# Last stage of an attention and two-layer kernel on one core: conversion steps a turn behind their producers, block sums in finer steps

## The chip, the core and the metric

The kernel runs on one core of a Trainium2 chip. A core has a matrix engine (TensorE, PE in the profile, with PEld for its weight loads), VectorE (DVE), ScalarE (ACT), GpSimd (POOL) and SyncE (SP, which here only issues DMAs). Each engine works through its own list of instructions in order, and waits at an instruction until the semaphores that it needs have been raised; what stands behind a waiting instruction on the same engine waits too. The metric is the device time of one execution in microseconds.

## What is computed

The reference is a block-causal attention (4 batches, 8 heads, 576 positions), a two-layer mixing network on its output, and a third part, which is the last stage of the kernel:

```python
xn = (x - mu) / np.sqrt(var + 1e-06) * g_ln
ch = np.maximum(xn @ w_ch1, 0.0) @ w_ch2
return (x + ch)
```

There `x` has 2304 rows of 512, `w_ch1` is 512 x 2048 and `w_ch2` 2048 x 512, all in float32. The reference draws `w_ch1` and `w_ch2` as float32 inputs, so the kernel has to prepare them on the chip.

## The kernel before, in words

Every matrix product is made with three passes: each float32 operand is split into a high part that PE takes as it is and a low part (the rest), and PE adds high x high, high x low and low x high.

The last stage takes `w_ch1` and `w_ch2` in 8 chunks of 256 hidden units (c = 0 to 7), with two weight buffers `W[c % 2]`. The rows are in five groups: four of 512 rows in two pairs, P = (0, 3) and Q = (2, 1), and a group Z of 256 rows (number 4). For a chunk and a group, `em_c1` makes the hidden units (PE into `ph` tiles in PSUM, five buffers; ACT writes the high part of `h1`, DVE the low part at line 659), and `em_c2` multiplies `h1` with `w_ch2` (PE into `po` tiles, three buffers) and adds on DVE into `acc` (line 818). `em_c2` of a group stands behind `em_c1` of the next one.

For a pair of 512-row groups `em_c1s` replaces the two `em_c1`: it makes the pair's products with seven block products in place of eight (42 matmuls of 512 columns where two `em_c1` take 48). It needs four block sums of the inputs (`SF[0]` to `SF[3]`, 1 MB each, made once for each pair by `sum_forms` on DVE, ACT and POOL) and four of the weights (`TF[c]`, made anew for each chunk by `forms`). There is room for one pair's sums, so they are written to DRAM (`s_scr`), and `reload(i)` fetches those of the next pair into `SF[i]` once PE has read it. Inside `em_c1s` the PSUM tile `b` is read by ACT (`act(z, b)`) and then added to by a later product, so PE waits for that read.

The weights come in through SP in four jobs a chunk (`load_split`): `load` (DMA of raw bytes into one of two `raw8` buffers, which `forms` takes turns in too), `above` and `below` (two ACT operations that take the exponent out; the tile `a1` of `above` has one buffer, which `bits` gives back), `expo` (a subtraction, on POOL in this stage), `bits` (DVE, line 134), `high` (ACT copy) and `low` (POOL subtraction). `Convert.step`, called by `tick` between PE's pieces, moves each job that is under way one step on and starts one; `expo` and `bits` are one step. A turn is what one such call emits.

The chunks run: c = 0 and 1 with `em_c1` throughout; c = 2 with `em_c1s` for P only and `em_c1` for Z and Q; from c = 3 on with `em_c1s` for both pairs and `em_c1` for Z between them. P's sums are made during c = 1, Q's during c = 2. The weights of chunk c + 1 are converted during chunk c. The lists of DMAs are the order of SP, which has one queue; the order of all engines is that in which the code emits.

Of the kernel before, what the change touches and what calls it, by code (L numbers as in the profile page):

```python
# [32 lines left out]
def attention_moe_kernel(ctx, tc, raw_d, dup_d, raw0_d, dup0_d, v_d, v0_d, msk_d, mz_d, vec_d, eye_d, wk_d, wv_d, wr_d, wc1_d, wc2_d, out_d):  # L33
# [181 lines left out]
    T = {}  # L215
# [371 lines left out]
    def chunk_jobs(c):  # L587
        L, kept = [], []
        for k in (0, 2):
            w = wc1_d[128 * k:128 * k + 256, CF * c:CF * c + CF].rearrange("(a p) n -> p a n", a=2)  # L590
            L.append(load_split(w, lambda i, k=k: W[c % 2][0][i][:, k:k + 2], kept))
        for k in range(2):
            r0 = CF * c + 128 * k
            L += pieces(wc2_d[r0:r0 + 128], lambda i: W[c % 2][1][i], k, DM)
        if c > 1:

            z = []

            def forms():
                (b11, b12), (b21, b22) = [[st["a2"].rearrange("p (a n) -> p a n", a=2)[:, :, o:o + 128] for o in (0, 128)] for st in kept]  # L600
                raw = stg2.tile([128, 4096], I8, name="raw8")
                z.append(raw.bitcast(F32).rearrange("p (i a n) -> p i a n", i=4, a=2))
                z1, z2, z3, z4 = [z[0][:, i] for i in range(4)]
                for out, in0, in1 in ((z1, b12, b11), (z3, b22, b12), (z2, b22, z1), (z4, b21, z2)):
                    tt(out=out, in0=in0, in1=in1, op=ALU.subtract)

            L[2][2] += (forms,)
            L[2][3] = (L[2][3], lambda: act(TF[c][0], z[0]))
            L[2][4] = (L[2][4], lambda: sub(nc.gpsimd, TF[c][1], z[0], TF[c][0]))
        return L  # L610
# [62 lines left out]
    def sum_forms(pr, pool):  # L673

        (g0, g1) = pr
        v, g = nc.vector, nc.gpsimd
        st = {}

        def block(G, h, k):
            return [x[:, k].bitcast(F32) for x in quarter(G, h)]  # L680

        def op(eng, out, in0, in1, op=ALU.subtract):
            eng.tensor_tensor(out=out, in0=in0, in1=in1, op=op)  # L683

        def temp(n):
            st[n] = pool.tile([128, 512], F32, name="t")
            return st[n]

        def split(i, k, z):
            act(SF[i][:, 0, k], z)  # L690
            sub(g, SF[i][:, 1, k], z, SF[i][:, 0, k])
            if k:
                nc.sync.dma_start(out=s_scr[PAIRS.index(pr), i], in_=SF[i].bitcast(F32))

        def both(a, b, how):
            op(g, temp("t"), a[1], b[1], how)
            op(v, temp("z"), a[0], b[0], how)

        def first(k):
            both(block(g1, 0, k), block(g1, 1, k), ALU.add)  # L700
# [12 lines left out]

        def fourth(k):
            x = st.pop("x")
            op(v, x, x, block(g0, 1, k)[1], ALU.add)
            split(3, k, x)

        def fifth(k):
            both(block(g0, 0, k), block(g1, 0, k), ALU.subtract)  # L720

        def sixth(k):
            z = st.pop("z")
            op(v, z, z, st.pop("t"), ALU.add)
            split(2, k, z)


        if pr == PAIRS[0]:
            return [
                lambda: fifth(0), lambda: (sixth(0), fifth(1)), lambda: (sixth(1), first(0)), lambda: second(0), lambda: third(0),  # L730
                lambda: (fourth(0), first(1)), lambda: second(1), lambda: third(1), lambda: fourth(1),
            ]
        return [
            lambda: first(0), lambda: second(0), lambda: third(0), lambda: (fourth(0), first(1)), lambda: second(1), lambda: third(1),
            lambda: (fourth(1), fifth(0)), lambda: (sixth(0), fifth(1)), lambda: sixth(1),
        ]

    def load_form(pr, i):
        nc.sync.dma_start(out=SF[i].bitcast(F32), in_=s_scr[PAIRS.index(pr), i])
# [1 line left out]
    def em_c1s(c, pr, nxt, prev, tick):  # L741
# [93 lines left out]
    with tc.manual_schedule():  # L835
# [301 lines left out]
        T["attention"] = True  # L1137
        Z = GORD[2]
        for x, G in enumerate(GORD):
            em_c1(0, G, lambda: norms(x))  # L1140
# [9 lines left out]
                em_c2(0, GORD[x - 1], (2, 3))  # L1150
            conv.some(cs[2])
        es_z.close()
        todo = 0, GORD[-1]
        work = {"sums": [], "wait": 0}

        def open_sums(pr):
            work["es"] = ExitStack()
            tz = opened(work["es"], "tz", 4, side=R)
            work["sums"] = sum_forms(pr, tz)

        def open_forms(*cc):
            work["ef"] = es_f if len(cc) > 1 else ExitStack()
            ft = opened(work["ef"], "ft", side=R)
            ta = tf_tiles(ft, "ta")
            for c in cc:
                TF[c] = ta

        def tick():
            if work["sums"]:
                work["sums"].pop(0)()  # L1170
                if not work["sums"]:
                    work["es"].close()
                    open_forms(*work["next"])
            if work["wait"]:
                work["wait"] -= 1
            else:
                conv.step()

        def group(c, G, todo):
            c0, G0 = todo  # L1180
# [7 lines left out]
            return c, G  # L1188

        for c in range(1, NC2):  # L1190
            pr = PAIRS[::1 - 2 * (c % 2)]
            if c == 1:
                conv.all()
                work["wait"], work["next"] = 8, (2,)
                open_sums(PAIRS[0])
            elif c == 2:
                work["wait"], work["next"] = 7, range(3, NC2, 2)
            conv = Convert(chunk_jobs(c + 1) if c + 1 < NC2 else [])
            if c == 1:
                for G in (0, 3, Z, 2, 1):  # L1200
                    todo = group(c, G, todo)
            else:
                c0, G0 = todo
                em_c1s(c, pr[0], pr[1] if c > 2 else None, lambda: em_c2(c0, G0, (0, 1, 2, 3)), tick)
                if c == 2:
                    del TF[2]
                    work["ef"].close()
                    open_sums(PAIRS[1])
                todo = group(c, Z, (c, pr[0][1]))
                if c == 2:  # L1210
                    for G in pr[1]:
                        todo = group(c, G, todo)
                    conv.all()
                    del XN[g3, 0], T["o1"]
                    es_o.close()
                    fo = opened(es_f, "fb")
                    tb = tf_tiles(fo, "tb")
                    for k in range(4, NC2, 2):
                        TF[k] = tb
                else:  # L1220
                    em_c1s(c, pr[1], None, lambda: em_c2(c, Z, (0, 1)), tick)
                    todo = c, pr[1][1]
            conv.all()
        em_c2(*todo, range(4))


# [64 lines left out]
```

## Time and profile before

| what | us |
|---|---|
| median of 3 runs (919.23 to 922.35) | 921.18 |
| the profiled execution: its own time | 920.21 |
| its span | 918.4 |
| PE busy, share of the span | 815.3, 89% |
| DVE busy | 557.6, 61% |
| ACT busy | 424.9, 46% |
| POOL busy | 353.1, 38% |

The span is what the profiler saw from the first to the last instruction; the execution's time is 1.8 us longer. Busy shares are means over all stages. The last stage's chunk 1 begins at 501.28 us and takes most of the second half of the span. In the rows below, `po` is the tile that `em_c2` fills, `ph` that of `em_c1` and `em_c1s`, `a` the tiles of a weight conversion, `raw` the bytes loaded for it, `t` and `s` the temporaries and results of the block sums, `ta` and `tb` the weight sums.

### The profile page before, as it was taken

The page shows a single profiled execution, that of the slowest core. Times are in us where ns is not written, and L with a number is a line of the kernel's source. Part 1 is how long each engine was busy: PE and PEld are TensorE (multiplying, and loading weights), DVE is VectorE, ACT ScalarE, POOL GpSimd, SP SyncE. Part 2 cuts the span into 40 slices and gives each one's busy share as a digit, 9 for nine tenths or more (in the row PEclk, how much of TensorE's full clock was granted, in tenths as well). Part 3 has the DMA queues.
Part 4 walks back from the last instruction along what each step waited for, and adds up shares of the span by engine and source line. Part 5 has one row for each costly group of instructions (what it writes and reads, how often), then busy time and mean ns, then how long its engine had stood idle before and what let it go on. Part 6 is the DMA issues. An engine that isn't in the chain of part 4 may idle for free.

```text
span 918.4 us, 10591 instructions
## 1 busy us (share of the span) xinstructions
PE 815.3 (89%) x3762; PEld 669.9 (73%) x3762; DVE 557.6 (61%) x996; ACT 424.9 (46%) x729; POOL 353.1 (38%) x291
## 2 busy tenths in 40 slices
PE   4987888899899999999999778981979799897998
PEld 3665666667689899889888666871868687686886
DVE  6898899987853432443865636544555645646544
ACT  6875877787754353355424223124232423324211
POOL 6789679846841100110232634155150402305000
PEclk9999999999999999999999998995989899898999
DMA  9995577415301100023421151042603307061242
GB/s 239 318 308 177 161 230 235 149 54 188 95 32 58 44 37 24 35 70 138 141 100 47 46 189 40 1 182 92 245 30 135 140 4 267 5 224 51 89 186 115
DMA packets 44100, 113.01 MB, mean 123 GB/s; under 512 B 3920, under 2 KB 18384, under 8 KB 40464
## 3 DMA queue, kind: packets, MB, share of 16 engines
q1 hardware_dynamic: 38576, 89.97, 28.7%
q0 software_dynamic: 5040, 20.01, 7.3%
q10 hardware_dynamic: 432, 2.36, 0.6%
q8 instruction: 30, 0.49, 0.2%
q14 instruction: 22, 0.18, 0.1%
HBM read 92.14 MB, written 20.19 MB: 122 GB/s over the span
## 4 chain that ended last, share of the span: by engine, by line
PE 48%; DVE 21%; ACT 11%; issue 6%; DMA 6%; POOL 6%; SPq 0%; ACTq 0%; DVEq 0%; POOLq 0%
PE ph L348 14%; PE po L348 11%; PE s L348 11%; PE p L348 11%; DVE a L134 5%; DVE part L403 4%; DMA raw<-in_w_ch_dram 4%; POOL a L130 3%; ACT r L41 2%; ACT a L41 2%; ACT e L41 2%; DVE QK L436 2%; POOL t L683 2%; DVE mix L516 1%; POOL s L44 1%
## 5 line engine op out<-in xcount | busy, mean ns | idle before, releaser
L348 PE MATMUL po<-c,h 128*128 128x512 f32 x864 | 219.3, 405 | 57.6 <-DVE acc L818 55.3
L348 PEld LDWEIGHTS po<-c,h 128*128 128x128 f32 x864 | 165.6, 194 | 100.2 <-DVE acc L818 62.7
L130 POOL TENSOR_TENSOR a<-a,a 128x512 int32<-128x512 int32 x36 | 46.1, 1282 | 181.6 <-ACT a L41 181.5
L348 PE MATMUL ph<-x,c 128*128 128x512 f32 (+1 forms) x504 | 107.6, 358 | 0.3 <-POOL c L44 0.3
L818 DVE TENSOR_TENSOR acc<-po,acc 128x512 f32<-128x512 f32 x144 | 94.4, 684 | 20.2 <-PE po L348 19.3
L348 PE MATMUL s<-x,wk 128*128 128x384 f32 x576 | 103.1, 338 | 2.1 <-DVE x L44 1.8
L348 PEld LDWEIGHTS s<-x,wk 128*128 128x128 f32 x576 | 101.4, 188 | 3.6 <-DVE x L44 2.1
L348 PE MATMUL p<-wv,k 128*128 128x512 f32 x432 | 99.7, 390 | 0.6 <-DVE k L44 0.6
L44 POOL TENSOR_TENSOR x<-mix,x 128x384 fp32r<-128x384 f32 x36 | 40.3, 1133 | 152.6 <-ACT x L41 149.4
L348 PEld LDWEIGHTS ph<-x,c 128*128 128x128 f32 x504 | 85.7, 195 | 15.6 <-POOL c L44 0.8
L41 ACT ACTIVATE a<-raw,ce 128x512 int32<-128x512 int8 (+1 forms) x80 | 57.4, 749 | 80.5 <-DVE a L134 53.4
L348 PE MATMUL p<-e,V 128*128 128x512 f32 (+4 forms) x320 | 94.3, 443 | 0.0
L348 PEld LDWEIGHTS p<-wv,k 128*128 128x128 f32 x432 | 80.8, 188 | 17.5 <-DVE k L44 1.0
L134 DVE SCALAR_TENSOR_TENSOR a<-raw,a 128x512 int32<-128x512 int32 x52 | 61.0, 1174 | 38.9 <-POOL a L130 37.5
L348 PEld LDWEIGHTS p<-e,V 128*128 128x128 f32 x320 | 57.5, 194 | 33.5 <-issue 28.4
L44 DVE TENSOR_TENSOR k<-a,k 128x768 fp32r<-128x768 f32 x24 | 23.7, 987 | 81.5 <-ACT a L41 81.5
L403 DVE TRANSPOSE_TENSOR_REDUCE part<-s 128x14 f32<-128x448 f32 (+4 forms) x160 | 65.1, 468 | 1.0
L41 ACT ACTIVATE u<-ph 128x512 f32<-128x512 f32 x33 | 19.7, 598 | 98.1 <-PE ph L348 94.2
L44 POOL TENSOR_TENSOR c<-a,c 128x512 fp32r<-128x512 f32 x32 | 41.6, 1302 | 36.0 <-ACT c L41 36.0
L41 ACT ACTIVATE e<-s 128x1536 f32<-128x1536 f32 (+1 forms) x34 | 48.4, 1423 | 11.7 <-PE s L348 8.6
L348 PE MATMUL s<-QK 128*128 128x512 f32 (+4 forms) x160 | 32.6, 337 | 22.9 <-DVE QK L436 22.6
L348 PE MATMUL s<-wr,x 128*128 128x512 f32 x216 | 51.0, 396 | 2.1 <-DVE x L44 2.0
(156 smaller groups left out, 1213.0 us busy)
## 6 DMA issues: line engine op xcount, KB each, us to landing
s<-s_scr SPq DMA_DIRECT2D x20, 1024.0 KB, 6.7
kq<-in_dup_dram POOLq DMA_DIRECT2D x15, 1088.0 KB, 6.1
raw<-in_raw_dram SPq DMA_DIRECT2D x32, 288.0 KB, 4.7
s_scr<-s SPq DMA_DIRECT2D x8, 1024.0 KB, 3.9
raw<-in_w_ch_dram SPq DMA_DIRECT2D x16, 511.6 KB, 3.5
raw<-in_w_ch_dram SPq DMA_DIRECT2D x32, 255.6 KB, 6.0
V<-in_v_dram SPq DMA_DIRECT2D x16, 320.0 KB, 6.0
x_scr<-r SPq DMA_DIRECT2D x18, 256.0 KB, 2.0
```

Source lines behind the costliest of these rows:

```text
L41: nc.scalar.activation(out=out, in_=in_, func=func, **kw)
L44: eng.tensor_tensor(out=out, in0=in0, in1=in1.bitcast(F32), op=ALU.subtract)
L130: (nc.gpsimd if T.get("attention") else nc.vector).tensor_tensor(out=a1.bitcast(I32), in0=whole(a1), in1=whole(a2), op=ALU.subtract)
L134: stt(out=st["a2"].bitcast(I32), in0=w3, scalar=5, in1=st["a1"].bitcast(I32), op0=ALU.logical_shift_right, op1=ALU.bitwise_or)
L348: nc.tensor.matmul(out=out, lhsT=lhsT, rhs=rhs, start=start, stop=stop, **kw)
L403: red(out=pt[0:kp, b0:b0 + w // 32, j], in_=v3(s[0:kp, o:o + w]), axis=AX.X, op=ALU.max, apply_transpose=True)
L436: lambda x=x: tt(out=v3(dst)[:, x:x + 16], in0=m[:, x:x + 16].unsqueeze(2).to_broadcast([32, 16, 32]), in1=s[64:96, 512:544].unsqueeze(1). ...
L516: stt(out=m[:, o:o + w], in0=XT[b][:, kk, q0:q0 + w], scalar=omm[:, c + kk:c + kk + 1], in1=y[:, o:o + w], op0=ALU.mult, op1=ALU.add)
L683: eng.tensor_tensor(out=out, in0=in0, in1=in1, op=op)
L818: tt(out=acc[i], in0=p, in1=acc[i], op=ALU.add)
```

## The change

The chunk's conversion is written out as a list of 12 turns, in which `expo`, `bits`, `high` and `low` of a job are emitted in a later turn than what they read; from c = 2 on the list is preceded by five empty turns in chunks 2 and 3. `expo` of chunk 1 runs on DVE instead of POOL (the flag `attention` is set later). The block sums become 12 steps for P in chunk 1 and six steps for half of Q in each of chunks 2 and 3. After each half of Q its four half sums (512 KB each) are written out, and the four halves of P's sums that were overwritten are read back. Chunk 3 therefore runs `em_c1s` for P only, like chunk 2, and `em_c1` for Q; from c = 4 on both pairs use `em_c1s` as before. One subtraction of each block sum moves from POOL to DVE. `em_c1s` has two more calls of `tick`: one after the second reload, and one between the two halves of the earlier group's `em_c2`.

```diff
         load, above, below, ...
+        t_high, t_low = lambda: act(TF[c][0], z[0]), lambda: sub(nc.gpsimd, TF[c][1], z[0], TF[c][0])
+        return [
+            [load[0], load[1]],
+            [above[0], below[0]],
+            [expo[0]],
+            [bits[0], above[1], below[1]],
+            [expo[1], high[0], load[2]],
+            [bits[1], above[2], below[2], low[0]],
+            [expo[2], high[1], load[3], low[1]],
+            [bits[2], forms, above[3], below[3]],
+            [expo[3], high[2], t_high],
+            [bits[3], t_low],
+            [high[3], low[2]],
+            [low[3]],
+        ]
...
-            if k:
-                nc.sync.dma_start(out=s_scr[PAIRS.index(pr), i], in_=SF[i].bitcast(F32))
-
-        def both(a, b, how):
-            op(g, temp("t"), a[1], b[1], how)
-            op(v, temp("z"), a[0], b[0], how)
+
+        def begin(n, a, b, how):
+            op(g, temp("t" + n), a[1], b[1], how)
+            op(v, temp("z" + n), a[0], b[0], how)
+
+        def end(n):
+            z = st["z" + n]
+            op(v, z, z, st.pop("t" + n), ALU.add)
+            return z
...
         def second(k):
-            z, a = st.pop("z"), block(g0, 0, k)
-            op(v, z, z, st.pop("t"), ALU.add)
-            split(0, k, z)
-            op(v, temp("y"), z, a[0])
-            op(g, st["y"], st["y"], a[1])
+            z = end("1")
+            op(v, temp("y"), z, block(g0, 0, k)[0])
+            split(0, k, st.pop("z1"))
 
         def third(k):
-            y = st.pop("y")
-            split(1, k, y)
-            op(v, temp("x"), block(g0, 1, k)[0], y)
+            op(v, st["y"], st["y"], block(g0, 0, k)[1])
+            split(1, k, st["y"])
...
+    def dma_sums(pr, out, k=slice(0, 2)):
+        for i in range(4):
+            m, s = s_scr[PAIRS.index(pr), i][:, :, k], SF[i][:, :, k].bitcast(F32)
+            nc.sync.dma_start(out=m if out else s, in_=s if out else m)
...
         prod(e, s_(3), bq(1, 1))
         reload(3)
+        tick()
         prod(b, s_(1), t_(1), False)
         reload(1)
...
-        prev()
+        for f in prev:
+            f()
+            tick()
...
         em_c2(c, g0, (0, 1))
+        tick()
         prod(b, quarter(g1, 1), t_(3), False)
         split(w, 0, b)
-        tick()
...
+        def open_sums(pr, *kk):
...
+            def done(k):
+                if pr == PAIRS[1]:
+                    dma_sums(pr, True, k)
+                    dma_sums(PAIRS[0], False, k)
+
+            for k in kk:
+                sums.extend(other(k) + chain(k) if pr == PAIRS[0] else chain(k) + other(k))
...
         def tick():
...
+            if sums:
+                sums.pop(0)()
+                if len(sums) == 1:
+                    sums.pop(0)()
+                    open_forms(*T["next"])
+            if turns:
+                for f in turns.pop(0):
+                    f()
...
+            if c + 1 < NC2:
+                turns += [[] for _ in range(5)] * (c in (2, 3)) + chunk_jobs(c + 1)
...
+            one, two = (Q, P) if c in (5, 7) else (P, Q)
+            em_c1s(c, one, two if c > 3 else None, [lambda ts=ts, x=todo: em_c2(*x, ts) for ts in ((0, 1), (2, 3))], tick)
+            if c < 4:
+                close_forms(c)
+                T["next"] = (c == 3, 3) if c == 2 else (True, 4, 6)
+                open_sums(Q, c - 2)
+            tick()
+            todo = group(c, Z, (c, one[1]))
+            if c < 4:
+                for G in Q:
                     todo = group(c, G, todo)
```

The first place is SP in chunk 2, from the second raw load on (`raw_4913` is chunk 3's second job after the change, `raw_5074` before it; `s_39xx` and `s_3740` are `SF[0]` to `SF[3]`). Before:

```order
L99 DMA raw_5074<-in_w_ch_dram 128x2045 [waits DMAHW4_49]
L693 DMA s_scr<-s_3740 128x2048 [waits Pool_49]
L101 DMA raw_5107<-in_w_ch_dram 128x4093 [waits DMAHW7_49,DMAHW0_49,DVE_49]
L101 DMA raw_5140<-in_w_ch_dram 128x4093 [waits DMAHW3_49,DMAHW2_49,DMAHW6_49,DVE_49,Activation_49]
L693 DMA s_scr<-s_3918 128x2048 [waits Pool_49]
```

And now:

```order
L99 DMA raw_4913<-in_w_ch_dram 128x2045 [waits DMAHW1_49,DVE_49]
L101 DMA raw_5021<-in_w_ch_dram 128x4093 [waits DMAHW6_49,DMAHW2_49,DMAHW7_49,DVE_49,Activation_49]
L751 DMA s_scr<-s_3916 256x1x512 [waits DMAHW3_49,Pool_49]
L751 DMA s_scr<-s_3917 256x1x512 [waits DMAHW4_49,Pool_49]
L751 DMA s_scr<-s_3918 256x1x512 [waits DMAHW5_49,Pool_49]
L751 DMA s_scr<-s_3740 256x1x512
L751 DMA s_3916<-s_scr 128x2x512 [waits DMAHW3_49]
L751 DMA s_3917<-s_scr 128x2x512 [waits DMAHW4_49,DMAHW0_49]
L751 DMA s_3918<-s_scr 128x2x512 [waits DMAHW5_49,DMAHW1_49]
L751 DMA s_3740<-s_scr 128x2x512 [waits DMAHW6_49,DMAHW2_49]
L101 DMA raw_5085<-in_w_ch_dram 128x4093 [waits DVE_49]
```

The chunk's fourth raw load stood ahead of the last store; it now stands behind four stores and four reads, of which the third read waits for the third store to have landed.

The second place is ACT in chunk 4's first `em_c1s`, with the raw loads of its first two jobs (`raw_5642`, `raw_5695` before; `raw_5643`, `raw_5646` now; `h<-u` and `u<-ph` are the steps of `em_c1s`). Before, from the last `act(z, b)` of the block on:

```order
L41 ACTIVATE u<-ph 128x512
L41 ACTIVATE h_5677<-u 128x512
L41 ACTIVATE a_5691<-raw_5642,ce 128x512
L41 ACTIVATE a_5693<-raw_5642,ce 128x512
L41 ACTIVATE h_5677<-ph 128x512
L41 ACTIVATE a_5724<-raw_5695,ce 128x512
```

And now:

```order
L41 ACTIVATE h_5606<-u 128x512
L41 ACTIVATE a_5662<-raw_5643,ce 128x512
L41 ACTIVATE a_5664<-raw_5643,ce 128x512
L41 ACTIVATE a_5700<-raw_5646,ce 128x512
L41 ACTIVATE a_5702<-raw_5646,ce 128x512
L41 ACTIVATE u<-ph 128x512
L41 ACTIVATE h_5704<-u 128x512
L41 ACTIVATE c_3929<-a_5664 128x512
L41 ACTIVATE a_5739<-raw_5720,ce 128x512
L41 ACTIVATE a_5741<-raw_5720,ce 128x512
L41 ACTIVATE h_5704<-ph 128x512
```

The exponent operations of the first two jobs have moved ahead of the last `act(z, b)`. On SP the two raw loads stand there behind two reloads now, where three stood before them.

## Rows read from the trace of the kernel before

**Rows 1.** Chain of waits, PE, 500 to 918.4 us: total us, times, longest

```profile
PE po L348 <- DVE acc L818: 55.3, 10, 23.1
```

**Rows 2.** PE in order of time: start us, us, instructions, [idle before <-releaser]

```profile
501.28 1.54 PE L348 MATMUL ph<-x,c 128*128 128x512 f32 x6
514.01 1.65 PE L348 MATMUL po<-c,h 128*128 128x512 f32 x6 [2.33 <-DVE acc L818]
569.63 2.92 PE L348 MATMUL ph<-x,c 128*128 128x512 f32 x12
639.97 2.93 PE L348 MATMUL po<-c,h 128*128 128x512 f32 x6 [23.07 <-DVE acc L818]
642.69 3.00 PE L348 MATMUL ph<-x,c 128*128 128x512 f32 x12
676.45 2.93 PE L348 MATMUL po<-c,h 128*128 128x512 f32 x6 [5.56 <-DVE acc L818]
697.68 2.92 PE L348 MATMUL ph<-x,c 128*128 128x512 f32 x12
751.81 2.91 PE L348 MATMUL ph<-x,c 128*128 128x512 f32 x12
806.51 2.92 PE L348 MATMUL ph<-x,c 128*128 128x512 f32 x12
861.33 2.91 PE L348 MATMUL ph<-x,c 128*128 128x512 f32 x12
```

**Rows 3.** End of the chain that ended last: start us, us, work

```profile
906.00 8.22 PE po L348 x36
```

**Rows 4.** Chunk 2's end, SP, POOL and DVE in order of time

```profile
633.55 0.33 SPq L693 DMA_DIRECT2D s_scr<-s  x1
632.26 1.26 POOL L44 TENSOR_TENSOR s<-t,s 128x512 fp32r<-128x512 f32 x1 [4.70 <-ACT s L41]
635.99 1.73 DVE L134 SCALAR_TENSOR_TENSOR a<-raw,a 128x512 int32<-128x512 int32 x1 [4.47 <-POOL a L130]
```

**Rows 5.** Chunk 4's reloads and first raw loads, SP and ACT

```profile
702.00 3.04 SPq L739 DMA_DIRECT2D s<-s_scr  x3
705.15 0.84 SPq L99 DMA_DIRECT2D raw<-in_w_ch_dram  x2
714.45 1.42 ACT L41 ACTIVATE a<-raw,ce 128x512 int32<-128x512 int8 x2 [0.50 <-DMA raw<-in_w_ch_dram]
```

**Rows 6.** The same DVE operation without and with POOL running beside it

```profile
619.20 0.69 DVE L134 SCALAR_TENSOR_TENSOR a<-raw,a 128x512 int32<-128x512 int32 x1 [7.67 <-POOL a L130]
552.04 1.75 DVE L134 SCALAR_TENSOR_TENSOR a<-raw,a 128x512 int32<-128x512 int32 x1 [1.63 <-POOL a L130]
551.96 1.28 POOL L44 TENSOR_TENSOR c<-a,c 128x512 fp32r<-128x512 f32 x1
```

**Rows 7.** Groups by line and shape, 501 to 918 us: busy, mean ns | idle

```profile
L41 ACT ACTIVATE a<-raw,ce 128x512 int32<-128x512 int8 x50 | 35.7, 751 | 69.5 <-DVE a L134 42.4 <-DMA raw<-in_w_ch_dram 26.5
L41 ACT ACTIVATE h<-u 128x512 fp32r<-128x512 f32 x33 | 20.9, 632 | 43.1 <-DVE u L777 17.7 <-DVE u L788 17.1 <-DVE u L797 8.3
L41 ACT ACTIVATE ta<-raw 128x1024 fp32r<-128x1024 f32 x4 | 4.2, 1047 | 0.0
L130 POOL TENSOR_TENSOR a<-a,a 128x512 int32<-128x512 int32 x26 | 33.3, 1281 | 170.1 <-ACT a L41 170.1
L44 POOL TENSOR_TENSOR ta<-raw,ta 128x1024 fp32r<-128x1024 f32 x4 | 11.5, 2863 | 0.0
L818 DVE TENSOR_TENSOR acc<-po,acc 128x512 f32<-128x512 f32 x132 | 86.3, 684 | 16.5 <-PE po L348 15.9
L683 DVE TENSOR_TENSOR t<-t,x 128x512 f32<-128x512 f32 x8 | 6.3, 788 | 0.1
```

**Rows 8.** The page's DMA issues: count, KB each, median us to landing

```profile
s<-s_scr SPq DMA_DIRECT2D x20, 1024.0 KB, 6.7
s_scr<-s SPq DMA_DIRECT2D x8, 1024.0 KB, 3.9
```

More of the change, by code (lines that the diff above doesn't have):

```diff
@@ L594, in chunk_jobs, with forms @@
             L += pieces(wc2_d[r0:r0 + 128], lambda i: W[c % 2][1][i], k, DM)
[L595 to L610, printed above, removed]
+        if c < 2:
+            return L
+        z = []
+        def forms():
+            (b11, b12), (b21, b22) = [[st["a2"].rearrange("p (a n) -> p a n", a=2)[:, :, o:o + 128] for o in (0, 128)] for st in kept]
+            raw = stg2.tile([128, 4096], I8, name="raw8")
+            z.append(raw.bitcast(F32).rearrange("p (i a n) -> p i a n", i=4, a=2))
+            z1, z2, z3, z4 = [z[0][:, i] for i in range(4)]
+            for out, in0, in1 in ((z1, b12, b11), (z3, b22, b12), (z2, b22, z1), (z4, b21, z2)):
+                tt(out=out, in0=in0, in1=in1, op=ALU.subtract)
+        load, above, below, expo, bits, high, low = [list(x) for x in zip(*[(l, a1, a2, x, b, h, w) for l, (a1, a2), (x, b), h, w in L])]
+        t_high, t_low = lambda: act(TF[c][0], z[0]), lambda: sub(nc.gpsimd, TF[c][1], z[0], TF[c][0])
[13 more added lines that the diff above has]
+        ]
     def chunk_tiles(p):
@@ L722, in sixth @@
         def sixth(k):
[L723 to L736, printed above, removed]
+            end("3")
@@ L738, in load_form, with chain, other @@
+            split(2, k, st.pop("z3"))
+        def chain(k):
+            return [lambda: first(k), lambda: second(k), lambda: third(k), lambda: fourth(k)]
+        def other(k):
+            return [lambda: fifth(k), lambda: sixth(k)]
+        return chain, other
+    def dma_sums(pr, out, k=slice(0, 2)):
+        for i in range(4):
+            m, s = s_scr[PAIRS.index(pr), i][:, :, k], SF[i][:, :, k].bitcast(F32)
+            nc.sync.dma_start(out=m if out else s, in_=s if out else m)
     def load_form(pr, i):
@@ L1135, in norms @@
                     ln_z(i, eng=nc.gpsimd if x == 2 else nc.vector)
-        T["attention"] = True
         Z = GORD[2]
@@ L1152, in attention_moe_kernel, with open_forms, close_forms @@
         es_z.close()
+        T["attention"] = True
         todo = 0, GORD[-1]
[L1154 to L1164, printed above, removed]
+        sums, turns = [], [[conv.step] for _ in range(2)]
+        def open_sums(pr, *kk):
+            es = ExitStack()
+            chain, other = sum_forms(pr, opened(es, "tz", 4, side=R))
+            def done(k):
[4 more added lines that the diff above has]
+                sums.extend(other(k) + chain(k) if pr == PAIRS[0] else chain(k) + other(k))
+                last = sums[-1]
+                sums[-1] = lambda last=last, k=k: (last(), done(k))
+            if pr == PAIRS[0]:
+                sums.append(lambda: dma_sums(pr, True))
+            sums.append(es.close)
+        def open_forms(last, *cc):
+            T["ef"] = es_f if last else ExitStack()
+            ta = tf_tiles(opened(T["ef"], "ft", side=R), "ta")
             for c in cc:
                 TF[c] = ta
+        def close_forms(c):
+            del TF[c]
+            T["ef"].close()
         def tick():
[L1169 to L1177, printed above, removed]
+            if sums:
[6 more added lines that the diff above has]
+                    f()
         def group(c, G, todo):
@@ L1190, in attention_moe_kernel @@
         for c in range(1, NC2):
-            pr = PAIRS[::1 - 2 * (c % 2)]
+            P, Q = PAIRS
             if c == 1:
[L1193 to L1198, printed above, removed]
-            if c == 1:
-                for G in (0, 3, Z, 2, 1):
+                T["next"] = False, 2
+                open_sums(P, 0, 1)
+                turns += [[], []]
@@ L1210, in attention_moe_kernel @@
[L1210 to L1222, printed above, removed]
@@ L1223, in attention_moe_kernel @@
-            conv.all()
+                em_c1s(c, two, None, [lambda: em_c2(c, Z, (0, 1))], tick)
+                todo = c, two[1]
+                tick()
+            if c == 3:
+                del XN[g3, 0], T["o1"]
+                es_o.close()
+                tb = tf_tiles(opened(es_f, "fb"), "tb")
+                TF[5] = TF[7] = tb
         em_c2(*todo, range(4))
```

22 lines of the change are left out of this document (10 added, 12 removed).

## The prediction

> **What bounds the kernel now.** I read the views from coarse to fine. The page says that PE is busy for 89% of the span, so what can be gained lies in PE's idle time, and the chain of waits says where that is: in the last stage PE waits almost only for `acc`, the DVE addition that gives back a `po` buffer, 55.3 us in ten waits [rows 1]. PE in order of time gives each chunk its length and shows the waits: small ones in chunk 1 (2.33 us at 514.01), 23.07 us at the end of chunk 2, and one of about 5 us in each of chunks 3 to 6 [rows 2]. Chunk 7, which converts nothing, has none.
>
> DVE isn't short of work time there. It stands in front of `bits`, which waits for POOL's `expo`, which waits for ACT's exponent operations, and the additions are queued behind. At chunk 2's end [rows 4] the last `bits` before PE goes on had waited 4.47 us for POOL, and POOL 4.70 us for ACT. In chunk 4 ACT waits for a raw load that stands behind reloads [rows 5].
>
> **What each chunk would take without waits.** The last 36 matmuls take 8.22 us, 0.228 us each; chunk 7 ends after the first 12 of them, at 908.74, and so takes 908.74 - 861.33 = 47.4 us [rows 2, 3]. By count it has 204 matmuls of 512 columns (46.6 us), so each `em_c1s` costs 0.4 beside its matmuls. Chunk 1 has 216 (halving Z's 24 small ones): 49.3 us. A chunk with one `em_c1s` has 210: 48.4. From the starts in [rows 2], chunk 1 takes 68.35 us (19.0 over), chunk 2 73.06 (24.7 over), chunk 3 54.99 (7.6 over), and chunks 4 to 6 together 163.65 (21.4 over). These 72.7 us are all that the change can win, and chunk 3 gives back 1.0 of it at once, since Q is done there with `em_c1` (6 more matmuls, less one 0.4).
>
> **Chunk 1.** `bits` gets its `expo` a turn earlier, P's sums have POOL's half ready a turn before DVE adds it, and no store stands before the raw loads on SP until the conversion is done. Most of the waits have no cause left. What remains: turns 8 to 10 carry two `bits`, four operations of the sums and three halves of `h1`, while PE needs only 1.4 us for each of Z's two halves. Following the queues through with [rows 7], DVE reaches the first `acc` of the `em_c2` that follows some 2.8 us after PE has filled its three buffers. After a wait PE may restart slowly: nothing was lost after the 2.33 us one (six matmuls in a row of 1.65), 1.35 us after the 23.07 us one (2.72 from 639.97 to 642.69 where 1.37 would do) [rows 2]. I take 0.7 here. Chunk 1: 49.3 + 3.5 = 52.8, **15.5 less**. Bounds: no wait (19.0 less), or two such waits (12 less).
>
> **Chunks 4 to 6.** Count from the chunk's start. The first reload is issued at 4.3 (702.00 - 697.68). Before, three reloads and the first raw load, 3.67 MB, had landed 12.4 us later, when ACT went on at 714.45 [rows 5]. Now two reloads stand ahead: 2.62 MB, by proportion 8.9, and 9.4 if 2 us of it don't scale; with 9.2 it has landed at 13.5. This is earlier than before, but the two exponent operations now stand on ACT ahead of the last `act(z, b)`, as the second place of the order shows. So: exponent operations of job 1 (two at 0.75) to 15.0, `expo` 1.28 to 16.3, `bits` 0.69 to 17.0; the exponent operations of job 2 need the one `a1` buffer that this `bits` gives back, so they run to 18.5, and `act(z, b)` (0.6) to 19.1 [rows 6, 7]. PE reaches the product that adds to `b` after 72 matmuls, at 16.8: it waits 2.3 us. A little later `h1`'s activation of that product stands behind the third job's exponent operations, and Z's second half needs the `ph` buffer of `b`: 1.4 more. With 0.7 for a slow restart a chunk takes 47.4 + 4.4 = 51.8, three 155.4: **8.3 less**. Bounds: no wait left (21.4 less); nothing won.
>
> **Chunk 2 and chunk 3 (now alike).** Up to the end of `em_c1s` (20.8 us) there is nothing but PE work. Then six turns carry half of Q's sums and the conversion. DVE has eight sum operations (0.69 to 0.79), two `bits`, four halves of `h1` and six `acc` in 14 us of PE work, and `bits` takes 1.75 where POOL runs beside it [rows 6, 7]. By the queues PE waits 2.4 us in group 1's `em_c2` and 1.6 in Z's follower.
>
> The costly place is the last raw load. On SP it now stands behind four stores and four reads (first place of the order). The third store needs POOL's part of `SF[2]`, the last step of the sums: `bits` of job 2 to 37.3, exponent operations to 38.8, an `h1` activation and its DVE half to 40.1, DVE's sum to 40.8, ACT's copy 0.63 to 41.5, POOL 1.28 to 42.8. From there two stores, four reads and the load go through: seven halves of a megabyte, 3.67 MB, the amount that took 12.4 us in [rows 5]; it lands at 55.2. ACT stands at this load meanwhile, with the `h1` activations of the next group behind it. After landing: exponent operations 1.5, `high` 0.6, `t_high` 1.05; then `t_low` on POOL 2.86 beside the last `bits`, which ends about 0.55 after it (553.79 against 553.24 in [rows 6]); the rest of `h1` 0.69, `acc` 0.68: 7.9 in all [rows 7]. PE goes on at 63.1, with six matmuls (1.4) and a slow restart (1.35) to the chunk's end at 65.9, 17.5 over. Chunk 2 wins **7.2**, chunk 3 loses **10.9**. Bounds for the load: in time for PE, so that only 4.0 + 0.7 are left over (53.1 a chunk); or all seven at the 6.7 us that a 1024 KB read takes [rows 8], 3.5 x 6.7 = 23.5 us. I take 12.4, because the same queue moved the same amount in that time, most of it into the same tiles.
>
> Chunk 0 gains a few tenths at most: `expo` of chunk 1 goes to DVE, which has no PE waiting for it there (the first PE wait in [rows 2] is that at 514.01), and if that cover is gone it costs four operations of about `bits`' 0.69. Chunk 7 and the end stay as they are. **Sum:** -15.5 - 7.2 + 10.9 - 8.3 = -20.1, from the profiled execution's 920.2 to 900.1; the median of the runs is 1.0 above that execution, so 901.
>
> **The rivals.**
> *The last load is in time.* My chain to 42.8 has eight links; if the sums run well ahead of it, the transfers are over when ACT comes. Chunks 2 and 3 then take 53.1: 2 x 12.8 less, 875. If ACT also doesn't hold `act(z, b)` in chunks 4 to 6, 3 x 4.4 less again: 862. For it speaks that PE, when it waits, gives the others time; against it, that SP runs its list in order and can't issue the reads before the stores have landed.
>
> *The shared port.* DVE takes 0.69 us for `bits` alone and 1.75 with POOL's subtraction beside it [rows 6]. Before, DVE's sums mostly started after POOL's part, which they waited for, and took 0.69 to 0.79; now they run beside POOL's subtractions and `expo`. If each of the seven operations that I left at its short time in a half of Q pays 1.06 more, DVE is 7.4 us later, and with half of it covered PE loses 3.7 in each of chunks 2 and 3, and as much in chunk 1: 912. The Trainium skill, "SBUF — State Buffer", section "Who interferes with whom", has it as a rule: a DVE instruction with two SBUF inputs and a GpSimd instruction that reads SBUF exclude each other for the whole of the one that came first. By that rule all the sums would pay, and the trace agrees for `bits`; the rows of the sums hardly show it, since they seldom met POOL.
>
> *Slower.* The seven transfers go at the read's median, 6.7 us for 1024 KB [rows 8]: the load lands at 66.3 instead of 55.2, and chunks 2 and 3 each take 11.1 more: 923. From a landing 11.5 us later than mine on, the change loses. For it speaks that the halves are cut into pieces of 2 KB and that stores and reads of the same DRAM mix; against it, that the median holds the wait behind earlier reloads in the same queue.
>
> *The steps aren't really apart.* `forms` and the exponent operations still stand in the same turn as the `bits` that they need. If chunks 4 to 6 keep their waits and chunk 1 half of its own, 901 + 8 + 8 = 917, no difference to speak of.
>
> **Numbers.** A difference within 0.3% is about what a measurement of this kernel can't tell from none. Forecast (waits of some 17 us in chunks 2 and 3, 890 to 911): 0.45. Last load in time, 875: 0.2; with the wait in chunks 4 to 6 gone, 862: 0.07. Shared port, 912: 0.13. Slower, 923 and more: 0.09. Not apart, 917 to 921: 0.06. Faster is thus 0.85; the same 0.07 and slower 0.08, since 0.01 of the slower case would end within 0.3% and is put there. The range 866 to 919 leaves out the slower case and the best one, 0.16.
>
> **What the profile will show.** Right: chunk 1 within 56 us with one wait of 2 to 4 us; chunks 2 and 3 alike, each with one PE wait of 9 to 14 us for `acc` near its end, while ACT waits for a raw DMA; chunks 4 to 6 near 52 us, with a PE wait for ACT at `b`. Wrong: PE waits under 4 us at the ends of chunks 2 and 3 (the load was in time), DVE sums of 1.2 us and more (the port), chunk 4 at 47 to 48 us (ACT didn't hold PE), or a chunk 2 of over 73 us.

## The result and the profile after

The changed kernel takes 906.79 us (median of 4 runs, 904.26 to 907.11), the kernel before 921.76 in the runs beside it: a ratio of 0.983, 95% interval 0.980 to 0.987. That is 15 us faster; forecast were 901 us, 20 faster, with a range of 866 to 919. The profiled execution took 904.26 us with a span of 902.5.

The first view is the chain of waits of PE, from 500 us to the end. It answers to [rows 1]:

```profile
PE po L348 <- DVE acc L836: 34.0, 7, 12.2
PE ph L348 <- ACT u L41: 8.8, 3, 3.2
```

The waits for `acc` have fallen from 55.3 to 34.0 us, and two of them make up most of it; a new kind, for ACT at a `ph` tile, has appeared three times. PE in order of time, with the starts of the chunks and the larger waits, answers to [rows 2]:

```profile
500.80 5.67 PE L348 MATMUL ph<-x,c 128*128 128x512 f32 x24
534.25 2.93 PE L348 MATMUL po<-c,h 128*128 128x512 f32 x6 [3.41 <-DVE acc L836]
556.54 2.92 PE L348 MATMUL ph<-x,c 128*128 128x512 f32 x12
620.01 2.93 PE L348 MATMUL po<-c,h 128*128 128x512 f32 x6 [12.22 <-DVE acc L836]
622.74 3.04 PE L348 MATMUL ph<-x,c 128*128 128x512 f32 x12
686.41 2.93 PE L348 MATMUL po<-c,h 128*128 128x512 f32 x6 [12.17 <-DVE acc L836]
689.14 3.91 PE L348 MATMUL ph<-x,c 128*128 128x512 f32 x12
710.29 1.73 PE L348 MATMUL ph<-x,ta 128*128 128x512 f32 x6 [3.09 <-ACT u L41]
711.81 4.46 PE L348 MATMUL po<-c,h 128*128 128x512 f32 x12
742.31 2.91 PE L348 MATMUL ph<-x,c 128*128 128x512 f32 x12
794.41 2.92 PE L348 MATMUL ph<-x,c 128*128 128x512 f32 x12
845.96 2.91 PE L348 MATMUL ph<-x,c 128*128 128x512 f32 x12
```

The chunks begin at 500.80, 556.54, 622.74, 689.14, 742.31, 794.41 and 845.96. Their lengths stand against the forecast like this (before: from [rows 2]):

| chunk | before | forecast | measured |
|---|---|---|---|
| 1 | 68.35 | 52.8 | 55.74 |
| 2 | 73.06 | 65.9 | 66.20 |
| 3 | 54.99 | 65.9 | 66.40 |
| 4 to 6 | 163.65 | 155.4 | 156.82 |
| sum | 360.05 | 340.0 | 345.16 |

The span fell by 15.9 us; the 1.0 that these chunks don't hold lies ahead of chunk 1 and in chunk 7, 0.5 each.

The next view is chunk 2's end in order of time, SP, POOL and ACT (start us, us, [idle before <-releaser]); it answers to [rows 4]:

```profile
586.59 14.06 SPq L751 DMA_DIRECT2D s_scr<-s  x4
600.70 4.08 SPq L751 DMA_DIRECT2D s<-s_scr  x4
604.83 0.63 SPq L101 DMA_DIRECT2D raw<-in_w_ch_dram  x1
598.15 1.29 POOL L44 TENSOR_TENSOR s<-t,s 128x512 fp32r<-128x512 f32 x1 [2.81 <-ACT s L41]
612.91 1.39 ACT L41 ACTIVATE a<-raw,ce 128x512 int32<-128x512 int8 x2 [13.83 <-DMA raw<-in_w_ch_dram]
```

The four stores take SP from 586.59 to 600.65, since the third waits for POOL's last low part (598.15 + 1.29); the four reads take it to 604.78, and only then does the fourth raw load go out. ACT stands for 13.83 us until 612.91, 56.4 us after the chunk's start (forecast: 55.2), and PE goes on at 620.01, 63.5 after the start (forecast: 63.1). In chunk 3 PE goes on 63.7 us after the start.

Chunk 4's start, SP and ACT, answers to [rows 5]:

```profile
694.47 1.71 SPq L754 DMA_DIRECT2D s<-s_scr  x2
696.24 1.84 SPq L99 DMA_DIRECT2D raw<-in_w_ch_dram  x4
704.79 1.39 ACT L41 ACTIVATE a<-raw,ce 128x512 int32<-128x512 int8 x2 [4.76 <-DMA raw<-in_w_ch_dram]
709.65 0.58 ACT L41 ACTIVATE u<-ph 128x512 f32<-128x512 f32 x1
```

The raw loads are issued behind two reloads, the exponent operations start at 704.79, 15.6 us after the chunk's start (forecast: 13.5), and `act(z, b)` is done at 710.23, where PE has waited 3.09 us for it.

### The profile page after: what moved, and what is told of

It is laid out like the page before. It is cut to its first block, busy times and chain, and to the rows that moved or that the text cites. A ratio compares the mean times of both kernels' runs of the same rounds, so it can differ in the third digit from the quotient of the medians.

```text
span 902.5 us, 10604 instructions
## 1 busy us (share of the span) xinstructions
PE 818.8 (91%) x3768; PEld 672.1 (74%) x3768; DVE 567.8 (63%) x1000; ACT 421.7 (47%) x726; POOL 350.2 (39%) x283
## 5 line engine op out<-in xcount | busy, mean ns | idle before, releaser
L348 PE MATMUL po<-c,h 128*128 128x512 f32 x864 | 216.8, 403 | 35.0 <-DVE acc L836 34.4
L348 PE MATMUL ph<-x,c 128*128 128x512 f32 (+1 forms) x528 | 112.5, 357 | 0.0
L348 PEld LDWEIGHTS ph<-x,c 128*128 128x128 f32 x528 | 89.1, 193 | 15.4
L348 PE MATMUL p<-e,V 128*128 128x512 f32 (+4 forms) x320 | 96.7, 451 | 0.0
L130 POOL TENSOR_TENSOR a<-a,a 128x512 int32<-128x512 int32 x32 | 43.9, 1371 | 126.7 <-ACT a L41 126.5
L44 POOL TENSOR_TENSOR c<-a,c 128x512 fp32r<-128x512 f32 x32 | 45.8, 1440 | 57.9 <-ACT c L41 57.9
L348 PE MATMUL s<-wr,x 128*128 128x512 f32 x216 | 52.8, 405 | 3.1 <-DVE x L44 3.0
L671 DVE SCALAR_TENSOR_TENSOR h<-ph,h 128x512 fp32r<-128x512 f32 (+1 forms) x40 | 23.2, 583 | 50.1 <-ACT h L41 50.1
```

The lines of the kernel that those rows point to most:

```text
L44: eng.tensor_tensor(out=out, in0=in0, in1=in1.bitcast(F32), op=ALU.subtract)
L130: (nc.gpsimd if T.get("attention") else nc.vector).tensor_tensor(out=a1.bitcast(I32), in0=whole(a1), in1=whole(a2), op=ALU.subtract)
L348: nc.tensor.matmul(out=out, lhsT=lhsT, rhs=rhs, start=start, stop=stop, **kw)
L671: stt(out=h1[1][:, m, 0:n], in0=p[:, 0:n], scalar=0.0, in1=h1[0][:, m, 0:n].bitcast(F32), op0=ALU.max, op1=ALU.subtract)
```

## The experiments

Each is the changed kernel with one edit, unless said otherwise; none leaves out work. Chunk lengths are from PE in order of time in each run's profile.

**The last raw load ahead of the sums' transfers.** The stores and reads of a half of Q are emitted behind the conversion's steps of their turn, so that the fourth raw load goes out first:

```diff
-                sums[-1] = lambda last=last, k=k: (last(), done(k))
+                sums[-1] = lambda last=last, k=k: (last(), later.append(lambda: done(k)))
...
                 for f in turns.pop(0):
                     f()
+            while later:
+                later.pop(0)()
```

> The changed kernel with the fourth raw load of chunks 2 and 3 issued ahead of the four stores and four reads of the half sums, all else alike. Theory (ACT stands at a raw load that stands behind the sums' transfers on SP): the 12.2 us PE waits at the ends of chunks 2 and 3 shrink to some 3 us, each chunk from 66.3 to 55 or 56, the time from 906.8 to about 885. Rival (DVE is late there anyway, because its sums meet POOL at the shared port): the load lands earlier, but PE still waits 8 us or more, and the time stays above 898.

Measured: 882.65 us, ratio to the kernel before 0.958 (0.955 to 0.960). SP, and PE's chunk starts with the last wait of chunk 2:

```profile
587.20 8.37 SPq L101 DMA_DIRECT2D raw<-in_w_ch_dram  x2
595.67 6.03 SPq L751 DMA_DIRECT2D s_scr<-s  x4
```

```profile
557.57 2.92 PE L348 MATMUL ph<-x,c 128*128 128x512 f32 x12
611.00 1.67 PE L348 MATMUL po<-c,h 128*128 128x512 f32 x6 [2.15 <-DVE acc L836]
612.51 2.91 PE L348 MATMUL ph<-x,c 128*128 128x512 f32 x12
```

SP now issues both loads of `w_ch2` in one stretch from 587.20 and the first store after them. The 12.2 us wait is one of 2.15, chunks 2 and 3 take 54.94 and 54.90 us. So the long wait came from the load's place on SP; DVE's own lateness is worth about 2 us here, not 8.

**The first raw loads ahead of the reloads (chunks 4 to 6).** The turn that stood behind the second reload now stands ahead of the first:

```diff
+        tick()
         prod(d, s_(0), t_(0))
         reload(0)
         prod(e, s_(3), bq(1, 1))
         reload(3)
-        tick()
```

> The changed kernel with the turn that loads a chunk's first two raw tiles emitted before the first reload of the block sums instead of after the second (chunks 4 to 6). Theory (the 2.5 to 3.2 us waits of PE for ACT come from the load's place behind 2 MB of reloads, since the exponent operations stand ahead of the read of b on ACT): these waits vanish, with the slow restart behind them 3 to 4.5 us a chunk, 10 to 13 in all: 894 to 897. Rival (the second job's exponent operations wait for the one a1 buffer, that is for bits, and hold ACT just as long): the waits stay above 2 us and the time within 3 us of 906.8.

Measured: 893.25 us, ratio 0.968 (0.966 to 0.971). PE's waits, then chunk 4 on SP and ACT:

```profile
PE po L348 <- DVE acc L836: 35.0, 9, 12.7
684.15 1.76 SPq L99 DMA_DIRECT2D raw<-in_w_ch_dram  x4
693.70 10.29 SPq L754 DMA_DIRECT2D s<-s_scr  x4
699.12 1.40 ACT L41 ACTIVATE a<-raw,ce 128x512 int32<-128x512 int8 x2
704.91 0.58 ACT L41 ACTIVATE u<-ph 128x512 f32<-128x512 f32 x1
```

The raw loads go out at 684.15, before chunk 4 starts at 688.65, and the reloads from 693.70. ACT takes the first exponent operations without a stop and `act(z, b)` at 704.91, 16.3 us after the chunk's start. PE has no wait for ACT left, and chunks 4 to 6 take 48.2, 47.5 and 47.8 us, close to the 47.4 of a chunk that converts nothing. The one `a1` buffer still makes ACT wait 3.08 us at 703.61, but that wait ends in time: the rival named in the expectation is out.

**`expo` on DVE.** The flag that sends the subtraction to POOL isn't set any more:

```diff
         es_z.close()
-        T["attention"] = True
```

> The changed kernel with the conversion's subtraction (expo) on DVE in all chunks, as it has it in chunk 1's weights, instead of POOL. If DVE's two-input operations and POOL's exclude each other, POOL loses 24 subtractions of 1.3 to 1.75 us, bits falls from a mean of 1.45 us towards 0.7 and the sums from 0.99 towards 0.7, chunk 1 falls from 55.7 to 52 or 53 and chunks 2 to 6 by 1 to 2 each: 896 to 901. If the port costs little on the path: DVE has 24 operations more, the time stays within 3 us of 906.8 or is longer.

Measured: 908.72 us, ratio 0.985 (0.983 to 0.987), within 2 us of the changed kernel. DVE's groups after the change (first) and with this edit (second): busy, mean ns, then idle before them.

```profile
L134 DVE SCALAR_TENSOR_TENSOR a<-raw,a 128x512 int32<-128x512 int32 x26 | 37.7, 1451 | 17.8 <-POOL a L130 17.6
L695 DVE TENSOR_TENSOR t<-t,x 128x512 f32<-128x512 f32 x12 | 11.6, 969 | 0.3
L695 DVE TENSOR_TENSOR t<-t 128x512 f32<-128x512 f32 x8 | 7.3, 909 | 0.0
```

```profile
L134 DVE SCALAR_TENSOR_TENSOR a<-raw,a 128x512 int32<-128x512 int32 x27 | 33.1, 1224 | 0.3
L130 DVE TENSOR_TENSOR a<-a,a 128x512 int32<-128x512 f32 x27 | 24.1, 892 | 34.4 <-ACT a L41 34.4
L695 DVE TENSOR_TENSOR t<-t 128x512 f32<-128x512 f32 x8 | 5.4, 681 | 0.0
```

DVE's sums rose from 0.79 [rows 7] to 0.97 us (`t<-t,x`) with the change. Without POOL's `expo`, `bits` falls from 1.45 to 1.22 and `t<-t` from 0.91 to 0.68 us, so both had met it; `t<-t,x` stays at 1.00. DVE waits 34.4 us for ACT at its own `expo`, which is 22.7 us more work for it. Chunk 1, for which the first theory named 52 or 53 us, takes 56.15; chunks 2 and 3 win 2.9 us each (63.3, 63.4), chunks 4 to 6 lose 7.7 together (55.4, 55.4, 53.8). So taking `expo` off POOL gives back as much as it wins; whether chunks 4 to 6 lose by DVE's waits for ACT or by its longer work, this run doesn't separate.

**The old order of steps in chunks 4 to 6.** The conversion of the weights of chunks 5 to 7 is written in the order of the kernel before, a job a turn:

```diff
+        if c > 4:
+            return [
+                [load[0]],
+                [above[0], below[0], load[1]],
+                [expo[0], bits[0], above[1], below[1], load[2]],
+                [high[0], expo[1], bits[1], above[2], below[2], load[3]],
+                [low[0], high[1], expo[2], bits[2], forms, above[3], below[3]],
+                [low[1], high[2], th, expo[3], bits[3]],
+                [low[2], tl, high[3]],
+                [low[3]],
+            ]
```

> The changed kernel with the conversion of chunks 5 to 7's weights (made in chunks 4 to 6) written in the old order: expo and bits of a job in one turn, high and low one turn behind, one job a turn; the extra turns in em_c1s and the place of the loads stay. If the separation of the steps is what shortened chunks 4 to 6, they go back from 52.3 to some 54.5 us with PE waits for acc in group Z's part: 913 to 915. If only the place of the loads and turns did it: 904 to 908.

Measured: 927.83 us, ratio 1.006 (1.004 to 1.009): slower than either side of the expectation. PE's first two waits in chunk 4, ACT between them, and who DVE's `bits` waited for in chunks 4 to 6:

```profile
710.92 1.66 PE L348 MATMUL po<-c,h 128*128 128x512 f32 x6 [3.07 <-DVE acc L848]
710.49 1.41 ACT L41 ACTIVATE a<-raw,ce 128x512 int32<-128x512 int8 x2 [2.35 <-DMA raw<-in_w_ch_dram]
716.98 2.93 PE L348 MATMUL ph<-x,ta 128*128 128x512 f32 x6 [4.41 <-ACT u L41]
DVE a L134 <- POOL a L130: 24.4, 9, 6.4
```

Chunks 4 to 6 take 58.8, 58.8 and 59.4 us, more than in the kernel before (54 to 55). The change also starts the conversion earlier within `em_c1s`, where PE needs DVE and ACT in every block; with `bits` waiting there for POOL (24.4 us in nine waits, against 11.0 in three in the changed kernel) PE waits for `acc` and for `b`. So the old list costs 6.7 us a chunk at this place, and some 4 us more than it took at its own. Not all of this is the separation of the steps: the list also loads one job a turn, its second raw load stands behind a third reload on SP (issued at 699.76), and ACT waits 2.35 us for it at 710.49. The run doesn't separate the two.

**Both moves.** The edits of the first two experiments together.

> Both of the moves that helped: the fourth raw load of chunks 2 and 3 ahead of the sums' transfers, and the first two raw loads of chunks 4 to 6 ahead of the reloads. If the two waits are independent, as the theory has it, the gains add up: 882.7 less 13.5, some 869. If one only took the place of the other (the later load or reload is late then), 876 or more.

Measured: 868.84 us, ratio 0.942 (0.940 to 0.944). The gains add up.

**The conversion of chunk 1 two turns later**, on top of both moves:

```diff
-                turns += [[], []]
+                turns += [[], [], [], []]
```

> As the kernel with both moves, and the conversion in chunk 1 two turns later, so that its turns with bits fall less in group Z's two short pieces of PE work. If the 3.4 us wait that is left in chunk 1 comes from DVE's work in those short turns, it goes below 1.5 us and the time by 2 to 4 us (866). If it is the sum of DVE's work over the chunk, the wait only moves to a later place: 868 to 871.

Measured: 872.01 us, ratio 0.945 (0.943 to 0.947), 3.2 us slower. The 3.4 us wait of chunk 1 becomes two, of 2.34 and 1.96; chunk 1 takes 56.96 against 55.86, and chunk 3, which starts at the lower clock here (granted 0.63 as a mean from 613.62 to 618.00), 1.5 more. ACT at the fourth raw load in chunk 1:

```profile
550.04 1.40 ACT L41 ACTIVATE a<-raw,ce 128x512 int32<-128x512 int8 x2 [6.52 <-DMA raw<-in_w_ch_dram]
```

The total is near the second line of the expectation (868 to 871), but its reason isn't shown: the first wait did shrink, and the second, at 557.21, has a cause of its own. With the conversion two turns later the fourth raw load goes out at 542.07, behind the four stores of P's sums (534.66 to 541.95), and ACT stands 6.52 us for it with `h1` activations behind it, the first of which DVE waits for 4.73 us.

**The sums' two halves in one turn.** POOL's part and DVE's addition of it are emitted together:

```diff
-            return [lambda: first(k), lambda: second(k), lambda: third(k), lambda: fourth(k)]
+            return [lambda: None, lambda: (first(k), second(k)), lambda: third(k), lambda: fourth(k)]
...
-            return [lambda: fifth(k), lambda: sixth(k)]
+            return [lambda: None, lambda: (fifth(k), sixth(k))]
```

> The changed kernel with the finer steps of the sums undone at one point: POOL's half of a sum and DVE's addition of it are emitted in the same turn (the turn before is left empty), twice for each half of a pair; the conversion's turns stay. If the sums' steps carry a good part of what chunk 1 gained (12.6 us), DVE stands for POOL's 1.3 us and more at each of the four places in chunk 1, PE waits there come back, chunk 1 goes from 55.7 to 58 or 60 and chunks 2 and 3 grow by 1 to 2 each: 910 to 915. If the conversion's steps and the stores' place alone made it: 905 to 908.

Measured: 909.50 us, ratio 0.986 (0.984 to 0.988). Chunk 1 takes 58.18 us, 2.4 more, chunks 2 and 3 67.3 and 69.4. The total lies just under the range that the first theory named; its places are where it said. Chunks 4 to 6, which the edit doesn't touch, take 3.3 us less: PE's waits for `b` are nearly the same there (2.68, 3.10, 2.65), but no slow restart follows them.

**The old order of steps in chunk 1.** The list of the fourth experiment for chunk 2's weights alone, behind five empty turns.

```diff
+        if c == 2:
+            return [[] for _ in range(5)] + [
+                [load[0]],
+                [above[0], below[0], load[1]],
+                [expo[0], bits[0], above[1], below[1], load[2]],
...
```

> The changed kernel with the one conversion that is made in chunk 1 (chunk 2's weights) written in the old order, expo and bits of a job in one turn and one job a turn, five turns later so that the weights' sums still come behind the block sums; the raw loads stay ahead of the stores of P's sums. If the separation of the steps carries the part of chunk 1's 12.6 us that the sums don't (they gave 2.5 when taken back), chunk 1 goes from 55.7 to 61 or more: 912 and more. If it was the stores' place behind the raw loads, chunk 1 stays within 2 us of 55.7: 905 to 909.

Measured: 915.08 us, ratio 0.994 (0.991 to 0.996). PE's last waits in chunk 1, then SP and ACT there:

```profile
551.48 4.42 PE L348 MATMUL po<-c,h 128*128 128x512 f32 x12 [3.18 <-DVE acc L848]
562.66 2.93 PE L348 MATMUL po<-c,h 128*128 128x512 f32 x6 [6.76 <-DVE acc L848]
540.42 3.74 SPq L763 DMA_DIRECT2D s_scr<-s  x4
544.71 0.61 SPq L101 DMA_DIRECT2D raw<-in_w_ch_dram  x1
555.64 1.39 ACT L41 ACTIVATE a<-raw,ce 128x512 int32<-128x512 int8 x2 [8.57 <-DMA raw<-in_w_ch_dram]
```

Chunk 1 takes 64.66 us, 8.9 more than with the steps apart, with waits of 3.18 and 6.76 us where the conversion lies. But the expectation is wrong in one point: the raw loads do not all stay ahead of the stores. The fourth goes out at 544.71, behind the four stores (1 MB each), ACT stands 8.57 us for it, `bits` waits 6.38 for POOL behind ACT, and the 6.76 us wait of PE follows. So this wait belongs to the load's place. Without it and its slow restart (1.35) the chunk would have taken some 56.5 us, an estimate, 0.8 more than with the steps apart; what the order of the steps costs alone the run doesn't show.

**The conversion's steps ahead of the sums' within a turn**, on top of the two moves and the two turns in chunk 1: `tick` takes its turn of the conversion first and its step of the sums after it.

```diff
+            if turns:
+                for f in turns.pop(0):
+                    f()
             if sums:
                 sums.pop(0)()
...
-            if turns:
-                for f in turns.pop(0):
-                    f()
```

> As the kernel with both moves and the later conversion in chunk 1, and within a turn the conversion's steps are emitted ahead of the sums' steps, so that expo doesn't stand behind a sum's low part on POOL. If the 2 us waits that are left in chunks 2 and 3 come from that order on POOL, each chunk wins 2 to 4 us: 861 to 865. If the sums then only come later by as much: within 2 us of the run without it.

Measured: 858.49 us, ratio 0.931 (0.929 to 0.932): 13.5 us faster than without it, more than expected, and the fastest version. POOL and DVE's `bits` of the first job in chunk 2, with both moves (first; the chunk starts at 556.75) and with this order (second; at 556.88):

```profile
581.54 1.30 POOL L44 TENSOR_TENSOR s<-t,s 128x512 fp32r<-128x512 f32 x1 [4.92 <-ACT s L41]
582.79 1.75 POOL L130 TENSOR_TENSOR a<-a,a 128x512 int32<-128x512 int32 x1
584.57 1.74 DVE L134 SCALAR_TENSOR_TENSOR a<-raw,a 128x512 int32<-128x512 int32 x1 [1.19 <-POOL a L130]
```

```profile
577.30 1.29 POOL L130 TENSOR_TENSOR a<-a,a 128x512 int32<-128x512 int32 x1 [0.55 <-ACT a L41]
582.24 1.28 DVE L134 SCALAR_TENSOR_TENSOR a<-raw,a 128x512 int32<-128x512 int32 x1
```

With the sums first, `expo` stands behind a low part that waits for ACT and starts at 582.79; `bits` follows at 584.57 and holds the additions. With the conversion first it starts at 577.30, and `bits` finds it done. Chunks 2 and 3 fall from 54.9 and 56.5 to 50.35 and 50.36 us. Chunk 1 falls from 56.96 to 55.04: there the new order also puts the fourth raw load ahead of the four stores again (532.63 and 539.76).

**One turn of delay in chunk 1 instead of two**, in that version.

```diff
-                turns += [[], [], [], []]
+                turns += [[], [], []]
```

> The fastest kernel so far (both moves, conversion steps ahead of the sums' steps within a turn, the conversion of chunk 1 two turns later) with that conversion one turn later instead of two. If the second turn of delay costs in chunk 1 what the pair of them cost without the new order within a turn (3 us), some 1.5 us less: 857. If chunk 1's end no longer hangs on it: 858 to 859.

Measured: 860.11 us, ratio 0.933 (0.931 to 0.935), 1.6 us above the run before, whose interval it overlaps; the wait in chunk 1 is 3.26 us again, against 2.33, and the chunk takes 57.15 against 55.04. Neither line of the expectation held: one turn less of delay wins nothing, and whether the second turn helps is not clear of the noise.

## Why the prediction came out as it did

**What bounds the kernel.** Right: PE's idle time in the last stage, and in it DVE behind `bits` behind POOL, is where the time came from. The page's busy shares of the other engines hardly moved. What DVE's `bits` waited for in chunk 1 of the kernel before (total us, times, longest):

```profile
DVE a L134 <- POOL a L130: 14.7, 6, 9.4
```

The block sums waited another 8.0 us for POOL's half there. In chunk 1 of the changed kernel neither wait is left.

**Chunk 1.** The mechanism was right and the size off: 52.8 forecast, 55.74 measured, 2.9 of the 5 us that are missing in the sum of the chunks. The term that was too small is the one wait of 2.8 with 0.7 for a slow restart: there are two waits, 0.69 and 3.41, and the restart cost its full 1.35 and 0.3 after it. The rest, some 0.7, no wait shows; the run of the second experiment, which had the same waits and no slow restart, took 54.25. The prediction followed the queues with DVE's operations at their short times. In front of the 3.41 us wait four sums take 5.88 us where they took some 2.8 before, with POOL busy beside them; one of them, and POOL's `expo` at that time:

```profile
524.97 1.76 DVE L695 TENSOR_TENSOR t<-t 128x512 f32<-128x512 f32 x1
524.89 1.29 POOL L130 TENSOR_TENSOR a<-a,a 128x512 int32<-128x512 int32 x1
```

Each of the four ends some 0.55 us after POOL's operation beside it. Of the 3.1 us more, at least 1.2 stand between DVE's last wait (until 529.08) and its `acc`. No run isolates them; if they are a part of the wait, that 2.8 came near 3.41 is partly luck.

Of the three reasons given for the win, POOL's half of the sums a turn ahead is worth 2.4 us by itself. The other two, the order of the conversion's steps and that no store stands before the raw loads, come to 8.9 us together. No run separates them, but what there is speaks for the loads: in the kernel before, the longest wait of `bits` (9.4) came after ACT had stood 8.27 us for a raw load issued behind the four stores, and in the two runs in which the fourth load came behind the stores again PE waited 6.76 and 1.96 us for it.

**Chunks 4 to 6.** Right to within 1.4 us in the sum, and by the cause named: the exponent operations stand at a load behind two reloads, ahead of the read of `b`. The second part of the term (1.4 us for the `ph` buffer of `b`) isn't there as a PE wait; the first is 2.5 to 3.2 us instead of 2.3: in chunk 4 the load landed 10.3 us after the first reload was issued (704.79 against 694.47) where 9.2 were forecast, and that reload went out 1.0 later in the chunk. The third term, 0.7 for a slow restart, was too small: 1.7 us were lost behind each of these waits (in chunk 4 the 12 matmuls from 711.81 take 4.46 us; 12 take 2.9 at the full clock), and 1.0 more at chunk 4's start, behind chunk 3's long wait. Over the three chunks the waits were 1.9 us longer than forecast, the second part 4.2 less and the restarts 4.0 more, so that the sum is near by luck, though the mechanism at `b` is right.

**Chunks 2 and 3.** Right by link: the third store at 43 us of the chunk (42.8), the landing at 56.4 (55.2), PE's return at 63.5 (63.1). The sizes of the two small waits were near too, 2.08 and 1.35 where 2.4 and 1.6 were forecast. The load took 13.5 us from the third store on instead of 12.4, and the work behind it 7.1 instead of 7.9. The rate chosen, that of the reloads before, was the right end of the bounds; the case "slower", with the read's median, would have had the load 10 us later. The case "load in time" is what the first experiment made: chunks 2 and 3 at 54.9 us where that rival had 53.1.

**The shared port.** As the reason of the long waits it is out, as a cost it is there. DVE's sums grew by some 0.2 us in their two largest groups, and three groups of two went from 0.68 to 0.74 us to 1.32 to 1.41, so the sign that the prediction named, sums of 1.2 us and more, came in part. The Trainium skill, "SBUF — State Buffer", section "Who interferes with whom", has it that a DVE instruction with two SBUF inputs and a GpSimd instruction that reads SBUF contend; the trace agrees, since the sum at 524.97 above ends 0.55 us after POOL's operation beside it. But the 3.7 us a chunk of that case did not come in chunks 2 and 3, which hung on the load; what it costs in chunk 1, no run isolates. Taking `expo` off POOL gave 2.9 us in each of chunks 2 and 3 and took it back in chunks 4 to 6.

**The steps aren't apart.** Out: the waits of `bits` for POOL are gone in chunk 1 (14.7 us before), and so are PE's waits for `acc` in chunks 4 to 6. What the separation is worth alone isn't shown: the two runs with the old list (8.9 us in chunk 1, 6.7 in each of chunks 4 to 6) moved raw loads too.

What the change wins is therefore 12.6 us in chunk 1, 6.9 in chunk 2 and 6.8 in chunks 4 to 6, less 11.4 in chunk 3, which now carries a half of Q's sums and the same late load as chunk 2. Three places in the order of emission (the last load behind the sums' transfers, the first loads behind the reloads, the sums' steps ahead of the conversion's within a turn) kept it from the 858 us that the same operations take, in a version that also delays chunk 1's conversion by two turns.

## What to carry to other kernels

When a wait is taken away by emitting steps later or earlier, follow each moved instruction on its own queue, the DMA queue above all: the largest cost here was one 0.5 MB load that came to stand behind eight transfers which themselves waited for the slowest chain of the stage. The same happened unseen in two experiments, which moved a step and with it a load behind four stores: read the queue's order again after each edit. And within a turn, put the step that others wait for first: a step that waits for another engine holds up what is emitted after it on its own engine.

## What the runs showed of the hardware that was not expected

The restart after a PE wait isn't a matter of its length alone. The same wait in chunk 1, where the two programs are alike, is followed by a granted clock of 0.50, 1.2 GHz, in the changed kernel, and by the full 2.4 GHz in the run with the first raw loads ahead of the reloads. Windows of both (columns: window, us, busy time of PE, PEld, DVE, ACT and POOL with counts, granted clock, DMA share and GB/s), and the wait of the second:

```profile
534.25:537.00 2.75, 2.75 (x7) 2.18 (x8) 2.75 (x3) 1.26 (x3) 1.72 (x2) 0.50 0.80 264
```

```profile
535.02:536.50 1.48, 1.48 (x6) 1.23 (x7) 1.48 (x3) 1.11 (x3) 1.48 (x2) 1.00 0.75 205
535.02 1.65 PE L348 MATMUL po<-c,h 128*128 128x512 f32 x6 [3.42 <-DVE acc L836]
```

PE had waited 3.41 us before the first and 3.42 us before the second, with the same work around it; the six matmuls behind the wait took 2.93 and 1.65 us. In three more runs with the same chunk 1 they took 2.93 again, behind 3.42 to 3.44 us. What decides it, these runs don't show; it moves a chunk by some 1.4 us, so that smaller differences between two chunks say little.
